# Second norm folded around w_in, w_mod's last columns loaded behind w_in, and wo loaded in plain rows: a cached attention and gMLP decode step

## Chip, cores, metric

One core of a Trainium2 chip runs the whole kernel. The metric is device time in microseconds of one execution; the median over several runs is given, and the profile is of one execution more.

## What is computed

A decode step for four sequences, one token each: an adaptive layer norm, attention over a cache of 4,096 positions in 32 heads, a second adaptive norm and a gated MLP. The shift, scale and gate of each half come from `silu(c) @ w_mod`, six vectors of 512.

```python
def _B_ref(x, w_in, w_sp, b_sp, w_out):
    z = _gelu(jnp.einsum('bsd,df->bsf', x, w_in))
    z1 = z[..., :Fh].copy()
    z2 = _layernorm(z[..., Fh:], axis=-1)
    g = jnp.einsum('ts,bsf->btf', w_sp, z2) + b_sp[None, :, None]
    return jnp.einsum('bsf,fd->bsd', z1 * g, w_out)

x = A_x
mod = (_silu(c) @ w_mod).reshape(c.shape[0], 6, 1, -1)
sa, ca, ga, sb, cb, gb = ...
h = _layernorm(x, axis=-1) * (1 + ca) + sa
x = x + ga * _A_ref(h, A_k_cache, A_v_cache, A_wq, A_wo)
h = _layernorm(x, axis=-1) * (1 + cb) + sb
x = x + gb * _B_ref(h, B_w_in, B_w_sp, B_b_sp, B_w_out)
```

All inputs are bf16. K and V are 4 x 32 x 4,096 x 128 each, 268 MB together; wo is 4,096 x 512, w_in 512 x 1,792, w_out 896 x 512, w_mod 512 x 3,072.

## The kernel before

**Order.** The order of instructions on each engine is that of the code; nothing is rescheduled. Nearly all transfers are issued by SP into one queue, in program order, and a load into a buffer that is still read waits there.

**Quads.** The 32 heads are taken in 8 groups of 4; a group and a sequence make a quad, 32 in all. The K of a quad (4 MB) lies as 128 partitions of 128 positions by 128 elements, and so does its V. Each has two buffers. Loop turn i loads K of quad i+1 and V of quad i, with wo's part for the group (512 KB) between the two at the first sequence of a group (L388). The last quad's K comes in two pieces and its V in four (L96).

**Scores.** DVE multiplies half a K tile by the query in place (L251), PE folds it with 16 matmuls against the identity (L256), DVE reduces and finds the maximum (L265 to L283), ACT takes the exponential (L286).

**Values.** For all quads but the last, PE multiplies V in blocks (L309), ACT copies (L315), PE takes the diagonal (L322). For the last quad, `values_last` has 128 matmuls of a 128x128 V block against four columns (L333) as V's pieces land, with three pairs of filler matmuls between (`keep_busy`, L127). The sum of the weights (`st["z"]`, L295) and the weighted values (`st["o"]`) are two halves of one PSUM tile, `zo`. `project` divides (L344, L345) and writes oT.

**wo.** Seven of the eight loads give each partition four rows in a row (`wo_w`, a run of 4 KB); `apply` then puts oT into that order with 16 small matmuls (L361) and a copy (L367) before it multiplies (L370). The eighth group has one row of 1 KB at a time (`wo_v`) and needs no such step. `apply` stands at the end of the loop turn.

**w_mod.** Vectors 0 and 1 are loaded at the start; 2 to 5 in turn 8 (L402, one load of 2 MB with runs of 4 KB) and multiplied in turn 10 (`mod_part`).

**The tail.** w_in (L431) and w_out (L433) are queued behind the last V. Then: x1 (L436, L437), the sums of x1 and its square by a matmul with a constant matrix (`ln_stats`, L147 to L165: DVE squares, PE sums, DVE takes mean and variance, ACT takes 1/std by Ln and Exp), a table load for GELU (L439), five fillers (L440), the norm in four DVE operations (L442 to L446), 56 matmuls with w_in (L453), one filler, GELU of both halves (L460, L464), a table load, the norm of z2 (`ln_stats` again), 28 matmuls with w_out (L471), the closing arithmetic (L476 to L490), a transposing matmul (L492) and the store (L497).

Of the kernel before, what the change touches and what calls it, by code (L numbers as in the profile page):

```python
# [8 lines left out]
BF16 = mybir.dt.bfloat16  # L9
# [7 lines left out]
def kernel(  # L17
# [75 lines left out]
        return load(A_k_cache, i, "kt", (2, 2) if i == len(quads) - 1 else (1,))  # L93

    def load_v(i):
        return load(A_v_cache, i, "vt", (2, 4, 8, 8) if i == len(quads) - 1 else (1,))  # L96

    NQ = len(quads)

# [22 lines left out]
    def keep_busy(n):  # L122

        if busy_ps[0] is None:
            busy_ps[0] = psum_s.tile([P, 4 * P], F32, name="big", bufs=2)
        for _ in range(n):
            nc.tensor.matmul(busy_ps[0], lhsT=ident, rhs=wide, start=True, stop=True)  # L127
# [40 lines left out]

    modT = persist.tile([P, 6, J, B], F32, name="modT")
    qbc = persist.tile([P, B, G, DH], BF16, name="qbc")  # L170
    x1b = persist.tile([P, 2, J, B], F32, name="x1b")
    wbf = persist.tile([P, 2], F32, name="wbf")
    xcT = persist.tile([P, J, 2 * B], F32, name="xcT")
# [8 lines left out]
        tc.tile_pool(name="psum_s", bufs=1, space=bass.MemoryType.PSUM)  # L182
    )

    def mod_part(wt, w0, oc):
        ps = psum_s.tile([P, J, B], F32, name="small", bufs=1)
        for jo in range(J):
            for j in range(J):
                c0 = (oc - w0) * D + jo * P
                nc.tensor.matmul(  # L190
                    ps[:, jo, :], lhsT=wt[:, j, c0:c0 + P],
                    rhs=sT[:, j, :], start=(j == 0), stop=(j == J - 1),
                )
        if oc in (1, 4):
            nc.vector.tensor_scalar_add(out=modT[:, oc], in0=ps, scalar1=1.0)
        else:
            nc.vector.tensor_copy(out=modT[:, oc], in_=ps)
# [46 lines left out]
    with tc.tile_pool(name="psum_att", bufs=1, space=bass.MemoryType.PSUM) as psum:  # L244
# [47 lines left out]
        def zsum(i):  # L292
            zo = psum.tile([P, 2, NH], F32, name="zo_ps", bufs=2)
            st["z", i], st["o", i] = zo[:, 0], zo[:, 1]
            nc.tensor.matmul(  # L295
                st["z", i], lhsT=ones_f, rhs=rs4s[i % NB], start=True, stop=True,
            )
# [29 lines left out]
        def values_last(i):  # L327
            P4 = P4s[i % NB]
            zsum(i)
            for n in range(NT):  # L330
                if n in (NT // 2, 3 * NT // 4, 7 * NT // 8):
                    keep_busy(2)
                nc.tensor.matmul(  # L333
                    st["o", i], lhsT=st["v", i][:, n, :], rhs=P4[:, n, :],
                    start=(n == 0), stop=(n == NT - 1),
                )

        def project(i):
            g, b = quads[i]
            if b == 0:  # L340
                st["oT", g] = wk.tile([P, NH, B], BF16, name="oT", bufs=2)
            oT = st["oT", g]
            rz = wk.tile([P, NH], F32, name="rz", bufs=2)
            nc.vector.reciprocal(out=rz, in_=st.pop(("z", i)))  # L344
            nc.vector.tensor_tensor(  # L345
                out=oT[:, :, b], in0=st.pop(("o", i)), in1=rz, op=ALU.mult,
            )
            if i == NQ - 1:
                apply(i)

        def apply(i):
            g, b = quads[i]
            if b == B - 1:
                oT = st.pop(("oT", g))
                wo_g = st.pop(("wo", g))
                if g < G - 1:

                    pp = psum_s.tile([P, NH, B], F32, name="small", bufs=1)
                    for r in range(NH):
                        for hl in range(NH):  # L360
                            nc.tensor.matmul(  # L361
                                pp[hl * R:(hl + 1) * R, r, :], lhsT=ident[:, r::NH],
                                rhs=oT[:, hl, :], start=True, stop=True,
                                tile_position=(0, hl * R),
                            )
                    oT = wk.tile([P, NH, B], BF16, name="oP", bufs=2)
                    nc.vector.tensor_copy(out=oT, in_=pp)  # L367
                for hl in range(NH):
                    for jo in range(J):
                        nc.tensor.matmul(  # L370
                            attn_ps[:, jo, :], lhsT=wo_g[:, hl, jo * P:(jo + 1) * P], rhs=oT[:, hl, :],
                            start=(g == 0 and hl == 0 and jo == 0),
                            stop=(g == G - 1 and hl == NH - 1),
                            skip_group_check=True,
                        )


        wo_w = A_wo.rearrange("(g p r) n -> g p r n", p=P, r=NH)
        wo_v = A_wo.rearrange("(g h p) n -> g p h n", h=NH, p=P)
        st["k", 0] = load_k(0)  # L380
        for i in range(NQ + 1):
            if i + 1 < NQ:
                st["k", i + 1] = load_k(i + 1)
            if i < NQ:
                if quads[i][1] == 0:
                    g = quads[i][0]
                    t = wk.tile([P, NH, D], BF16, name="wo_g", bufs=2)
                    nc.sync.dma_start(out=t, in_=(wo_v if g == G - 1 else wo_w)[g])  # L388
                    st["wo", g] = t
                st["v", i] = load_v(i)  # L390
                if i == 0:
                    wq_r = kvp.tile([P, J, (G - 1) * GW], BF16, name="wt", bufs=1)
                    nc.sync.dma_start(out=wq_r, in_=wq_v[:, :, GW:])
                if i in (2, 3):
                    for b in (2 * i - 4, 2 * i - 3):
                        for g0, n in ((1, 3), (4, 4)):
                            qp = psum_s.tile([P, n, DH], F32, name="big", bufs=2)
                            query(wq_r, 1, b, g0, n, qp, 0)
                            nc.scalar.copy(out=qbc[:, b, g0:g0 + n, :], in_=qp)  # L399
                if i == 8:  # L400
                    wm25 = kvp.tile([P, J, 4 * D], BF16, name="wt", bufs=1)
                    nc.sync.dma_start(out=wm25, in_=wmod_v[:, :, 2 * D:])  # L402
                if i == 10:
                    for oc in range(2, 6):
                        mod_part(wm25, 2, oc)
            if i > 1:
                diagonal(i - 2)
            if i < NQ:
# [7 lines left out]
            if i < NQ:  # L416
                fold(i, 0)
                fold(i, 1)
                softmax(i)
            if 1 < i < NQ:  # L420
                apply(i - 2)
        keep_busy(3)
        values_last(NQ - 1)
        project(NQ - 1)
# [1 line left out]

    with tc.tile_pool(name="post", bufs=1) as post, \
            tc.tile_pool(name="psum_post", bufs=1, space=bass.MemoryType.PSUM) as psum:
        wt = kvp.tile([P, J * F + JF * D], BF16, name="wt", bufs=1)
        win = wt[:, 0:J * F].rearrange("p (j n) -> p j n", j=J)  # L430
        nc.sync.dma_start(out=win, in_=B_w_in.rearrange("(j p) n -> p j n", p=P))  # L431
        wout = wt[:, J * F:].rearrange("p (j n) -> p j n", j=JF)
        nc.sync.dma_start(out=wout, in_=B_w_out.rearrange("(p j) n -> p j n", j=JF))  # L433

        x1 = x1b[:, 0]
        nc.vector.tensor_tensor(out=x1, in0=attn_ps, in1=modT[:, 2], op=ALU.mult)  # L436
        nc.vector.tensor_tensor(out=x1, in0=x1, in1=xT, op=ALU.add)  # L437
        mean, rstd = ln_stats(post, psum_s, x1b, mean_d, J, "ln2")
        nc.scalar.preload_act_table_set("gelu_apprx_tanh_and_others")  # L439
        keep_busy(5)  # L440
        h2 = post.tile([P, J, B], F32, name="h2")
        nc.vector.tensor_tensor(out=h2, in0=x1, in1=bc(mean, J), op=ALU.subtract)  # L442
        nc.vector.tensor_tensor(out=h2, in0=h2, in1=bc(rstd, J), op=ALU.mult)
        nc.vector.tensor_tensor(out=h2, in0=h2, in1=modT[:, 4], op=ALU.mult)
        h2T = post.tile([P, J, B], BF16, name="h2T")
        nc.vector.tensor_tensor(out=h2T, in0=h2, in1=modT[:, 3], op=ALU.add)  # L446


        z_ps = psum.tile([P, 2, JF, B], F32, name="zf_ps")
        for s in (1, 0):  # L450
            for jf in range(JF):
                for j in range(J):
                    nc.tensor.matmul(  # L453
                        z_ps[:, s, jf, :], lhsT=win[:, j, s * FH + jf:(s + 1) * FH:JF],
                        rhs=h2T[:, j, :], start=(j == 0), stop=(j == J - 1),
                    )
        keep_busy(1)
        z2b = post.tile([P, 2, JF, B], F32, name="z2b")
        z2 = z2b[:, 0]
        nc.scalar.activation(out=z2, in_=z_ps[:, 1], func=AF.Gelu_apprx_tanh)  # L460


        u = post.tile([P, JF, 2, B], BF16, name="u")
        nc.scalar.activation(out=u[:, :, 1, :], in_=z_ps[:, 0], func=AF.Gelu_apprx_tanh)  # L464
        nc.scalar.preload_act_table_set("natural_log_exp_and_others")
        mean, rstd = ln_stats(post, psum_s, z2b, mean_f, JF, "ln3", lambda:
            nc.vector.tensor_tensor(out=u[:, :, 0, :], in0=u[:, :, 1, :], in1=z2, op=ALU.mult))
# [20 lines left out]
        )  # L488
        yo = post.tile([P, B, J], BF16, name="yo")
        nc.vector.tensor_tensor(out=yo.rearrange("p b j -> p j b"), in0=q, in1=r1, op=ALU.add)  # L490
        t_ps = psum.tile([J * B, P], F32, name="t_ps")
        nc.tensor.matmul(  # L492
            t_ps, lhsT=yo.rearrange("p b j -> p (b j)"), rhs=ident, start=True, stop=True,
        )
# [33 lines left out]
```

## Time and profile before

| | |
|---|---|
| Runs | 675.93, 676.19, 676.55, 676.57; median 676.37 us |
| Profiled execution | 675.76 us, span 674.0 us |
| Instructions | 7,199 |
| Busy: PE / PEld / DVE / ACT | 62% / 31% / 56% / 15% |
| HBM read | 282.73 MB, 419 GB/s over the span |
| Chain that ended last, by engine | DMA 61%, PE 25%, DVE 12% |
| Granted TensorE clock, mean | 0.765 |
| K, V, wo to landing, median | 26.0, 34.3, 25.8 us |

The span is the time from the first instruction to the last of the profiled execution; 1.76 us of its own time lie around it. The median of the runs is 0.61 us above it. PE is TensorE, PEld its weight loads, DVE VectorE, ACT ScalarE, SP the engine that issues transfers; L12 is line 12 of the kernel before.

### The profile page before, as it was taken

The page shows a single profiled execution, that of the slowest core. Times are in us where ns is not written, and L with a number is a line of the kernel's source. Part 1 is how long each engine was busy: PE and PEld are TensorE (multiplying, and loading weights), DVE is VectorE, ACT ScalarE, POOL GpSimd, SP SyncE. Part 2 cuts the span into 40 slices and gives each one's busy share as a digit, 9 for nine tenths or more (in the row PEclk, how much of TensorE's full clock was granted, in tenths as well). Part 3 has the DMA queues.
Part 4 walks back from the last instruction along what each step waited for, and adds up shares of the span by engine and source line. Part 5 has one row for each costly group of instructions (what it writes and reads, how often), then busy time and mean ns, then how long its engine had stood idle before and what let it go on. Part 6 is the DMA issues. An engine that isn't in the chain of part 4 may idle for free.

```text
span 674.0 us, 7199 instructions
## 1 busy us (share of the span) xinstructions
PE 418.7 (62%) x3091; PEld 207.4 (31%) x3095; DVE 376.7 (56%) x408; ACT 102.9 (15%) x311; POOL 4.1 (1%) x18
## 2 busy tenths in 40 slices
PE   2574847765657656567666457765546766555786
PEld 2232423322224222233222223332223322223344
DVE  2665555566653666545656555565645565654732
ACT  1012211101111011111011111101111101111112
POOL 2000000000000000000000000000000000000000
PEclk9976888766778667788767788776678876768885
DMA  9999999999999999999999999999999999999993
GB/s 374 425 418 431 433 435 426 429 432 427 434 431 425 428 429 434 429 433 434 431 424 429 432 433 436 422 434 425 430 433 433 432 431 430 433 422 427 432 409 126
DMA packets 14256, 283.20 MB, mean 420 GB/s; under 512 B 1416, under 2 KB 2448, under 8 KB 5776
## 3 DMA queue, kind: packets, MB, share of 16 engines
q1 hardware_dynamic: 14144, 282.73, 98.2%
q8 instruction: 24, 0.39, 0.2%
q14 instruction: 8, 0.07, 0.0%
q10 hardware_dynamic: 16, 0.01, 0.0%
q0 software_dynamic: 64, 0.00, 0.0%
HBM read 282.73 MB, written 0.00 MB: 419 GB/s over the span
## 4 chain that ended last, share of the span: by engine, by line
DMA 61%; PE 25%; DVE 12%; issue 0%; ACT 0%; SPq 0%; DVEq 0%; ACTq 0%
DMA kt<-in_A_k_cache_dram 61%; PE s_ps L256 23%; DVE kt L251 11%; PE big L127 1%; PE zo_ps L333 0%; PE zf_ps L453 0%; ACT P L286 0%; PE big L309 0%; PE small L149 0%; PE y_ps L471 0%; DVE S L265 0%; ACT osb L315 0%; PE attn_ps L370 0%; PE zo_ps L295 0%; SPq L75 0%
## 5 line engine op out<-in xcount | busy, mean ns | idle before, releaser
L256 PE MATMUL s_ps<-kt,ident 128*128 128x512 bf16 x1024 | 291.9, 455 | 214.1 <-DVE kt L251 214.1
L251 DVE TENSOR_TENSOR kt<-kt,qbc 128x8192 bf16<-128x8192 bf16 x64 | 282.6, 4418 | 127.9 <-DMA kt<-in_A_k_cache_dram 127.9
L256 PEld LDWEIGHTS <-ident 128*128 128x128 bf16 x1024 | 115.7, 113 | 378.0 <-issue 225.0
L265 DVE TENSOR_REDUCE S<-s_ps 128x64 f32<-128x512 f32 x64 | 44.2, 691 | 126.5 <-PE s_ps L256 126.5
L315 ACT COPY osb<-big 128x512 f32<-128x512 f32 x31 | 18.2, 586 | 518.9 <-PE big L309 518.9
L286 ACT ACTIVATE P<-S,nm 32x128 bf16<-32x128 f32 x128 | 73.5, 574 | 20.3 <-DVE nm L283 18.0
L309 PE MATMUL big<-vt,P 128*32 128x512 bf16 x992 | 59.2, 380 | 0.0
L322 PE MATMUL zo_ps<-sel,osb 128*128 128x4 f32 x248 | 33.7, 259 | 16.4 <-ACT osb L315 16.4
L322 PEld LDWEIGHTS zo_ps<-sel,osb 128*128 128x128 f32 x248 | 31.1, 197 | 28.5 <-ACT osb L315 27.3
L286 ACT ACTIVATION_READ_ACCUMULATOR P<-S,nm 32x1 f32 x128 | 31.8, 248 | 0.0
L309 PEld LDWEIGHTS <-P 128*32 128x32 bf16 x992 | 23.7, 96 | 20.8
L295 PEld LDWEIGHTS zo_ps<-rs,ones_f 128*128 128x128 f32 x64 | 12.1, 190 | 5.6 <-ACT P L286 1.2
L204 PE MATMUL big<-wt,hbc 128*32 128x384 bf16 (+1 forms) x128 | 8.5, 404 | 3.8 <-ACT qbc L399 3.7
L344 DVE RECIPROCAL rz<-zo_ps 128x4 f32<-128x4 f32 x32 | 5.6, 176 | 9.1 <-PE zo_ps L333 7.3
L273 DVE TENSOR_REDUCE mx<-S 128x1 f32<-128x128 f32 x32 | 9.2, 286 | 1.3
L295 PE MATMUL zo_ps<-rs,ones_f 128*128 128x4 f32 x64 | 9.1, 212 | 0.7 <-ACT P L286 0.7
L204 PEld LDWEIGHTS <-hbc 128*32 128x32 bf16 x192 | 5.7, 113 | 10.7 <-issue 7.0
L283 DVE STREAM_TRANSPOSE nm<-hb 128x32 f32<-128x32 f32 x32 | 6.8, 212 | 3.2
L275 DVE STREAM_TRANSPOSE mT<-mx 128x32 f32<-128x32 f32 x32 | 6.8, 211 | 1.1
L277 DVE TENSOR_REDUCE hm<-mT 128x1 f32<-128x32 f32 x32 | 6.0, 186 | 1.1
L279 DVE TENSOR_SCALAR hb<-hm 128x32 f32<-128x32 f32 x32 | 5.8, 181 | 1.1
L345 DVE TENSOR_TENSOR oT<-zo_ps,rz 128x4 bf16<-128x4 f32 x32 | 5.4, 168 | 1.1
(92 smaller groups left out, 75.9 us busy)
## 6 DMA issues: line engine op xcount, KB each, us to landing
kt<-in_A_k_cache_dram SPq DMA_DIRECT2D x31, 4096.0 KB, 26.0
vt<-in_A_v_cache_dram SPq DMA_DIRECT2D x31, 4096.0 KB, 34.3
wo_g<-in_A_wo_dram SPq DMA_DIRECT2D x8, 512.0 KB, 25.8
kt<-in_A_k_cache_dram SPq DMA_DIRECT2D x2, 2048.0 KB, 24.2
wt<-in_A_wq_dram SPq DMA_DIRECT2D x1, 3584.0 KB
wt<-in_w_mod_dram SPq DMA_DIRECT2D x1, 2048.0 KB, 38.2
vt<-in_A_v_cache_dram SPq DMA_DIRECT2D x1, 2048.0 KB, 18.9
wt<-in_B_w_in_dram SPq DMA_DIRECT2D x1, 1792.0 KB
```

The source lines that it names most:

```text
L204: nc.tensor.matmul(qp[hl * R:(hl + 1) * R, col:col + n], lhsT=hbc[:, j, b, :], rhs=wv[:, g0 - hl0:g0 - hl0 + n, hl, :], start=(j == 0), st ...
L251: nc.vector.tensor_tensor(out=kt, in0=kt, in1=q[:, None, :].to_broadcast([P, HT, DH]), op=ALU.mult,)
L256: nc.tensor.matmul(ps, lhsT=ident, rhs=kt[:, :, cc * DC:(cc + 1) * DC], start=(cc == 0), stop=(cc == DH // DC - 1),)
L265: nc.vector.tensor_reduce(out=st["S", i][:, half * HT:(half + 1) * HT], in_=st.pop(("s", i, half)), axis=AX.X, op=ALU.add,)
L273: nc.vector.tensor_reduce(out=mx[:, 0:1], in_=S, axis=AX.X, op=ALU.max)
L275: nc.vector.transpose(out=mT, in_=mx)
L283: nc.vector.transpose(out=nm, in_=hb)
L286: nc.scalar.activation(out=P4[rows, 0:NT, hl], in_=S[rows, :], func=AF.Exp, bias=nm[rows, 0:1], scale=att_scale, accum_out=rs4[rows, hl:hl ...
L295: nc.tensor.matmul(st["z", i], lhsT=ones_f, rhs=rs4s[i % NB], start=True, stop=True,)
L309: nc.tensor.matmul(po[32 * t:32 * t + 32], lhsT=P4[:, n0:n0 + 8, :], rhs=st["v", i][:, n0:n0 + 4, :], start=(u == 0), stop=(u == NU - 1), ...
L315: nc.scalar.copy(out=osb, in_=po)
L322: nc.tensor.matmul(st["o", i], lhsT=osb[:, n, :], rhs=sel[:, NH * n:NH * n + NH], start=(n == 0), stop=(n == 3),)
```

## The change

wo is loaded in plain rows for all groups; the permutation goes, and the 16 matmuls with wo move into `project`. The last V comes in five pieces, and its denominator has a PSUM tile of its own. w_mod's vector 5 is no longer loaded in turn 8 but behind w_in, which comes in two halves, the second half of the columns first. The second norm is not applied to h ahead of w_in: w_in is multiplied with three sets of columns, x1(1+scale), 1+scale and shift, and mean and 1/std are applied to the products, `((a - mean*b) * rstd) + c`, for each half. The fillers of the tail go.

```diff
-        return load(A_v_cache, i, "vt", (2, 4, 8, 8) if i == len(quads) - 1 else (1,))
+        return load(A_v_cache, i, "vt", (2, 4, 8, 16, 16) if i == len(quads) - 1 else (1,))
...
+    hx = persist.tile([P, J, 3, B], BF16, name="hx")
...
-    def mod_part(wt, w0, oc):
-        ps = psum_s.tile([P, J, B], F32, name="small", bufs=1)
+    def mod_part(wt, w0, oc, ps=None):
+        if ps is None:
+            ps = psum_s.tile([P, J, B], F32, name="small", bufs=1)
...
             st["z", i], st["o", i] = zo[:, 0], zo[:, 1]
+            if i == NQ - 1:
+                st["z", i] = psum_s.tile([P, NH], F32, name="small", bufs=1)
...
-                if n in (NT // 2, 3 * NT // 4, 7 * NT // 8):
-                    keep_busy(2)
+                if n in (NT // 2, 3 * NT // 4, 7 * NT // 8, 15 * NT // 16):
+                    keep_busy(2 if n < 7 * NT // 8 else 1)
...
-            if i == NQ - 1:
-                apply(i)
-
-        def apply(i):
-            g, b = quads[i]
             if b == B - 1:
-                oT = st.pop(("oT", g))
                 wo_g = st.pop(("wo", g))
-                if g < G - 1:
-
-                    pp = psum_s.tile([P, NH, B], F32, name="small", bufs=1)
-                    for r in range(NH):
-                        for hl in range(NH):
-                            nc.tensor.matmul(
-                                pp[hl * R:(hl + 1) * R, r, :], lhsT=ident[:, r::NH],
-                                rhs=oT[:, hl, :], start=True, stop=True,
-                                tile_position=(0, hl * R),
-                            )
-                    oT = wk.tile([P, NH, B], BF16, name="oP", bufs=2)
-                    nc.vector.tensor_copy(out=oT, in_=pp)
                 for hl in range(NH):
...
-                    nc.sync.dma_start(out=t, in_=(wo_v if g == G - 1 else wo_w)[g])
+                    nc.sync.dma_start(out=t, in_=wo_v[:, g * NH:(g + 1) * NH, :])
...
-                    wm25 = kvp.tile([P, J, 4 * D], BF16, name="wt", bufs=1)
-                    nc.sync.dma_start(out=wm25, in_=wmod_v[:, :, 2 * D:])
+                    wm24 = kvp.tile([P, J, 3 * D], BF16, name="wt", bufs=1)
+                    nc.sync.dma_start(out=wm24, in_=wmod_v[:, :, 2 * D:5 * D])
                 if i == 10:
-                    for oc in range(2, 6):
-                        mod_part(wm25, 2, oc)
+                    for oc in range(2, 5):
+                        mod_part(wm24, 2, oc)
+                    nc.vector.tensor_copy(out=hx[:, :, 1, :], in_=modT[:, 4])
+                    nc.vector.tensor_copy(out=hx[:, :, 2, :], in_=modT[:, 3])
...
-            if 1 < i < NQ:
-                apply(i - 2)
...
-        nc.sync.dma_start(out=win, in_=B_w_in.rearrange("(j p) n -> p j n", p=P))
+        win_v = B_w_in.rearrange("(j p) n -> p j n", p=P)
+        for s in (1, 0):
+            nc.sync.dma_start(
+                out=win[:, :, s * FH:(s + 1) * FH], in_=win_v[:, :, s * FH:(s + 1) * FH],
+            )
+        wm5 = wt[:, J * F + JF * D:].rearrange("p (j n) -> p j n", j=J)
+        nc.sync.dma_start(out=wm5, in_=wmod_v[:, :, 5 * D:])
+        wout = wt[:, J * F:J * F + JF * D].rearrange("p (j n) -> p j n", j=JF)
         nc.sync.dma_start(out=wout, in_=B_w_out.rearrange("(p j) n -> p j n", j=JF))
...
-        mean, rstd = ln_stats(post, psum_s, x1b, mean_d, J, "ln2")
-        nc.scalar.preload_act_table_set("gelu_apprx_tanh_and_others")
-        keep_busy(5)
-        h2 = post.tile([P, J, B], F32, name="h2")
-        nc.vector.tensor_tensor(out=h2, in0=x1, in1=bc(mean, J), op=ALU.subtract)
-        nc.vector.tensor_tensor(out=h2, in0=h2, in1=bc(rstd, J), op=ALU.mult)
-        nc.vector.tensor_tensor(out=h2, in0=h2, in1=modT[:, 4], op=ALU.mult)
-        h2T = post.tile([P, J, B], BF16, name="h2T")
-        nc.vector.tensor_tensor(out=h2T, in0=h2, in1=modT[:, 3], op=ALU.add)
...
+        nc.vector.tensor_tensor(out=hx[:, :, 0, :], in0=x1, in1=hx[:, :, 1, :], op=ALU.mult)
+        zp = {}
+
+        def z_half(s):
+            zp[s] = psum.tile([P, JF, 3, B], F32, name=f"z{s}_ps")
             for jf in range(JF):
                 for j in range(J):
                     nc.tensor.matmul(
-                        z_ps[:, s, jf, :], lhsT=win[:, j, s * FH + jf:(s + 1) * FH:JF],
-                        rhs=h2T[:, j, :], start=(j == 0), stop=(j == J - 1),
+                        zp[s][:, jf], lhsT=win[:, j, s * FH + jf:(s + 1) * FH:JF],
+                        rhs=hx[:, j], start=(j == 0), stop=(j == J - 1),
                     )
-        keep_busy(1)
+
+        def z_norm(s):
+            t = post.tile([P, JF, B], F32, name=f"zn{s}")
+            nc.vector.tensor_tensor(out=t, in0=zp[s][:, :, 1, :], in1=bc(mean, JF), op=ALU.mult)
+            nc.vector.tensor_tensor(out=t, in0=zp[s][:, :, 0, :], in1=t, op=ALU.subtract)
+            nc.vector.tensor_tensor(out=t, in0=t, in1=bc(rstd, JF), op=ALU.mult)
+            nc.vector.tensor_tensor(out=t, in0=t, in1=zp[s][:, :, 2, :], op=ALU.add)
+            return t
+
+
+        z_half(1)
+        mean, rstd = ln_stats(post, psum_s, x1b, mean_d, J, "ln2")
+        nc.scalar.preload_act_table_set("gelu_apprx_tanh_and_others")
+        z_half(0)
+        mod_part(wm5, 5, 5, psum.tile([P, J, B], F32, name="m5_ps"))
...
-        nc.scalar.activation(out=z2, in_=z_ps[:, 1], func=AF.Gelu_apprx_tanh)
+        nc.scalar.activation(out=z2, in_=z_norm(1), func=AF.Gelu_apprx_tanh)
...
-        nc.scalar.activation(out=u[:, :, 1, :], in_=z_ps[:, 0], func=AF.Gelu_apprx_tanh)
+        nc.scalar.activation(out=u[:, :, 1, :], in_=z_norm(0), func=AF.Gelu_apprx_tanh)
...
-        t_ps = psum.tile([J * B, P], F32, name="t_ps")
+        t_ps = psum_s.tile([J * B, P], F32, name="small", bufs=1)
```

More of the change, by code (lines that the diff above doesn't have):

```diff
@@ L375, in apply @@
                         )
-        wo_w = A_wo.rearrange("(g p r) n -> g p r n", p=P, r=NH)
-        wo_v = A_wo.rearrange("(g h p) n -> g p h n", h=NH, p=P)
+        wo_v = A_wo.rearrange("(h p) n -> p h n", p=P)
         st["k", 0] = load_k(0)
@@ L428 @@
             tc.tile_pool(name="psum_post", bufs=1, space=bass.MemoryType.PSUM) as psum:
-        wt = kvp.tile([P, J * F + JF * D], BF16, name="wt", bufs=1)
+        wt = kvp.tile([P, J * F + JF * D + J * D], BF16, name="wt", bufs=1)
         win = wt[:, 0:J * F].rearrange("p (j n) -> p j n", j=J)
-        nc.sync.dma_start(out=win, in_=B_w_in.rearrange("(j p) n -> p j n", p=P))
-        wout = wt[:, J * F:].rearrange("p (j n) -> p j n", j=JF)
+        win_v = B_w_in.rearrange("(j p) n -> p j n", p=P)
[6 more added lines that the diff above has]
+        wout = wt[:, J * F:J * F + JF * D].rearrange("p (j n) -> p j n", j=JF)
         nc.sync.dma_start(out=wout, in_=B_w_out.rearrange("(p j) n -> p j n", j=JF))
@@ L437 @@
         nc.vector.tensor_tensor(out=x1, in0=x1, in1=xT, op=ALU.add)
-        mean, rstd = ln_stats(post, psum_s, x1b, mean_d, J, "ln2")
-        nc.scalar.preload_act_table_set("gelu_apprx_tanh_and_others")
-        keep_busy(5)
-        h2 = post.tile([P, J, B], F32, name="h2")
-        nc.vector.tensor_tensor(out=h2, in0=x1, in1=bc(mean, J), op=ALU.subtract)
-        nc.vector.tensor_tensor(out=h2, in0=h2, in1=bc(rstd, J), op=ALU.mult)
-        nc.vector.tensor_tensor(out=h2, in0=h2, in1=modT[:, 4], op=ALU.mult)
-        h2T = post.tile([P, J, B], BF16, name="h2T")
-        nc.vector.tensor_tensor(out=h2T, in0=h2, in1=modT[:, 3], op=ALU.add)
-        z_ps = psum.tile([P, 2, JF, B], F32, name="zf_ps")
-        for s in (1, 0):
+        nc.vector.tensor_tensor(out=hx[:, :, 0, :], in0=x1, in1=hx[:, :, 1, :], op=ALU.mult)
+        zp = {}
+        def z_half(s):
+            zp[s] = psum.tile([P, JF, 3, B], F32, name=f"z{s}_ps")
             for jf in range(JF):
```

## The prediction

> **What bounds the kernel now.** I read the slices of the page first, then the chain of waits, then the timeline of its last 40 us, then the DMA landings and packets.
>
> ```profile
> DMA  9999999999999999999999999999999999999993
> GB/s 374 425 418 431 433 435 426 429 432 427 434 431 425 428 429 434 429 433 434 431 424 429 432 433 436 422 434 425 430 433 433 432 431 430 433 422 427 432 409 126
> ...
> q1 hardware_dynamic: 14144, 282.73, 98.2%
> ```
>
> The DMA engines are full in 39 of 40 slices at about 430 GB/s, so up to some 655 us time is bytes and packets, and an instruction saved on PE or DVE there is worth nothing. What counts is when the last K and V tiles land and what follows them. The chain, in order of time (start, us, what), shows that:
>
> ```profile
> 591.74 27.34 DMA kt<-in_A_k_cache_dram
> ...
> 653.57 0.39 PE zo_ps L295 x2
> ...
> 659.93 0.20 DVE rz L344
> 660.13 0.02 issue
> 660.15 0.18 DVE oT L345
> ...
> 661.39 0.18 DVE x1b L147
> 661.57 0.04 issue
> 661.62 0.63 PE small L149 x2
> 662.25 2.13 PE big L127 x5
> 664.38 2.96 PE zf_ps L453 x56
> 667.34 0.02 issue
> 667.37 0.20 ACT z2b L460
> 667.57 0.02 issue
> 667.59 0.20 DVE z2b L147
> 667.79 0.04 issue
> 667.84 0.68 PE small L149 x2
> ```
>
> K of the last quad but one lands at 619.08; from there compute runs unbroken to the output. So the sum has two parts: how far the change moves that landing (the whole chain moves with it), and what it does to the tail after 653.57. In the tail the transfers run just ahead of their users: the last V piece lands at 635.7+22.6 = 658.3, w_in at 662.73 (landing event), w_out at 636.64+28.3 = 664.9.
>
> **Rows and packets ahead of the landing.** The packet records give a median of 46 ns for 1,024 B, 84 for 2,048, 142 for 3,584, 160 for 4,096, 1,215 for 32,768; 16 engines work side by side. A load of wo is 512 KB. With 4 KB rows it lands 1.26 to 1.28 us after the K tile ahead of it in the queue (four pairs with nothing between); the eighth load already has 1 KB rows and takes 1.48 (K 598.18, wo 599.66). So each of the seven loads that change costs +0.21, in all +1.47. Packet means (32 x 49.0 against 8 x 161.2 ns per engine) give +0.28 each, +1.96: the upper end; medians give 7 x 0.19 = +1.34, the lower. I take 1.47, the same form measured landing to landing.
>
> w_mod in the middle: 2 MB of 4 KB rows is 32 x 160 ns = 5.1 us per engine; 1.5 MB in 3 KB rows, which no record shows, lies between 84 and 160 ns a packet, on the line between them 122: 32 x 122 = 3.9. That is -1.21 (bounds -2.4 and 0). The landing of K and all behind it moves by +1.47 - 1.21 = **+0.26**. The extra V piece turns 8 packets of 160 into 16 of 84 per engine: +0.06, last V at 658.6.
>
> The Trainium skill, "DMA: Bandwidth & Descriptors", section "Why small descriptors are slow", puts the overhead of a packet at a fixed three or so bus cycles, 32 B a cycle. By that a 1 KB packet loses 3 in 35 and a 4 KB one 3 in 131, and a wo load would grow by only some 0.09 us (an estimate); the sum would be 0.8 us better than mine. The landing at 599.66 says 0.21, and the row decides.
>
> **The permutation that goes.** L361 (112 matmuls) and L367 (7 copies of 0.175) leave PE and DVE; the 16 matmuls of L370 move ahead of the second half's scores. I cost both at nothing: PE is busy 62% under a full queue. They wait on oT (L345), which DVE writes before its second multiplication, while PE still does the first half's matmuls (3.5 us and more). Without that cover it is 16 x 0.026 = 0.4 us in every fourth quad.
>
> **Last V.** Six filler matmuls stay six (2+2+1+1 for 2+2+2), 128 matmuls stay: PE-bound from 653.57 to 659.91, as pieces land before their use (658.3 against 659.3). The denominator in its own bank lets L344 run at 654: the 0.20 of rz with its issue leaves the chain, **-0.22**.
>
> **The tail.** Times in the changed kernel, with +0.26 and -0.22 in. After x1 one more DVE operation, hx, takes the place of L147 in the chain: it starts at 661.43, z_half(1) at 661.66 (0.23 later, as from L147 to L149). Its 28 matmuls go at 53 ns each ((3.12-0.19)/55 from L453): 1.49. Twelve columns for four: L471 with eight goes at 28 ns and L370 with four at 26, so the columns cost little, +0.1 to 0.2 at worst. The sums (L149) stand behind them on PE: 663.15, and z_half(0) starts 0.47 later (as L471 after L149), 663.62, to 665.11. Then mod_part, 16 x 0.026 + 0.16 = 0.58: 665.69. Meanwhile st, msq, var on DVE and two ACT operations end by 665.0. DVE has the copy of modT[5] next in its order, and all of z_norm stands behind it: copy at 665.73, four dependent operations at 0.22 each (L476 to L480) from 665.82, GELU at 666.70, second z_norm from 666.57, GELU at 667.46. DVE squares z2 at 667.32 and PE sums at 667.57. In the profile above PE sums at 667.84: **-0.27** in all, so the tail alone gives -0.31. z2 is earlier by 0.67, u is not: eight DVE operations replaced three and five fillers, and waits for the norm went under matmuls. Behind that nothing changes.
>
> The transfers in it: w_in in two halves of 1,792 B rows, about 75 ns a packet on the line between 46 and 84: 64 x 75 = 4.8 for 32 x 142 = 4.5, so with the 4.44 that w_in took by its landing, 4.66. Halves land at 660.9 and 663.3 (wanted 661.66, 663.62), the last w_mod columns 1.48 later at 664.75 (wanted 665.11), w_out 666.9 (wanted 668.0). All in time, two by 0.35 only.
>
> The fillers at L442's place go too. What covers that: the clock below is at half in the whole stretch although they ran (the columns are busy time and instructions of PE, PEld, DVE, ACT, POOL, then PEclk, DMA share, GB/s).
>
> ```profile
> 654.40:674.00 19.60, 12.97 (x225) 9.78 (x224) 4.22 (x24) 3.85 (x8) 0.00 (x0) 0.50 0.41 164
> ```
>
> GELU now follows its table load more closely. Before, the second load begins at 667.66 and the next ACT operation starts 1.53 later:
>
> ```profile
> 667.66 1.28 ACT L465 ACT_TABLE_LOAD   x1
> ...
> 669.19 0.30 ACT L164 ACTIVATE rstd_ln<-var_ln,eps 128x4 f32<-128x4 f32 x1 [0.24 <-DVE var_ln L162]
> ```
>
> By that row a load begun at 665.0 is over by 666.5, before GELU at 666.70. The Trainium skill, "ScalarE: Activation LUTs", section "What ACT_TABLE_LOAD costs", counts 2.66 us for a switch, a drain included. By it GELU would start at 667.66, and the end would be some 0.4 later than before instead of 0.27 earlier; the row above, where the next operation starts after 1.53, speaks against it.
>
> **Sum.** +0.26 - 0.22 - 0.31 = -0.27: span 674.00 to 673.73, profiled run 675.76 to 675.49. The median shown, 676.37, lies 0.61 over that run, so **676.1**. A measurement of this kernel can't tell less than 0.2%, 1.35 us, from no change: no measurable difference. Its own range is 675.3 to 677.1: wo between 1.34 and 1.96, twelve columns up to +0.2 in each half, the two thin margins of 0.35.
>
> **Rivals.** *B, slower: the last gate's columns come late.* In place: DVE's copy of modT[5] ahead of all of z_norm. It decides once those columns land after 665.1; from there each us of lateness is a us of time. Price with every packet at its worst row: wo +1.96 (landing +0.75), w_in at the 101 ns that 2 KB packets averaged at the kernel's start, 64 x 101 = 6.46, the columns 32 x 56 = 1.79. They land at 658.29+0.81+6.46+1.79 = 667.35, PE is ready at 665.6: 676.37 - 0.53 + 0.75 + 1.75 = **678.3**. For it: three more transfers stand in the queue, and SP sits 10.47 us in one issue there, so the queue takes no more than so much:
>
> ```profile
> 636.64 10.47 SPq L433 DMA_DIRECT2D wt<-in_B_w_out_dram  x1
> ```
>
> If the issue of the late transfers stays behind the drain, they start late too. Against it: a full queue is a busy queue, and that transfer landed in its turn, 2.18 after w_in.
>
> *C, faster: the 1 KB rows cost nothing.* Then only w_mod's -1.21 and the tail count: 676.37 - 1.21 - 0.53 = **674.6**. For it: the whole rate is within 1% in all slices. Against: the 1.48 of the eighth load.
>
> *D, the clock.* PE begins the last K at 638.77 with the clock at half until 644.16. If the changed kernel meets that switch one stretch of 3.4 us earlier or later, it gains or loses half of it: 674.4 or 677.8. Against it: the four runs before lie within 0.64.
>
> **How the numbers follow.** A 0.52, B 0.26, C 0.14, D 0.08 with both signs alike. So faster 0.18, same 0.52, slower 0.30. The time is A's, 676.1. The range 674.7 to 677.9 holds A and D nearly whole and the near parts of B and C, which reach toward A as their conditions hold in part.
>
> **What would show it.** The K landing near 619.3; wo loads at 1.5 us behind K; rz done before L345's wait ends; GELU of z2 near 666.7 and DVE's square near 667.3, with modT[5]'s copy released by PE and PE not by a DMA. It is wrong if mod_part waits for its transfer, if GELU waits for the table, or if K lands outside 618.9 to 619.9.

## The result, and the profile after

The changed kernel takes 676.91 us (median of 39 runs, 676.74 to 677.49) against 675.93 (57 runs, 675.12 to 676.94): a ratio of 1.0015, 95% interval 1.0011 to 1.0020. It is slower by 1.0 us, where 0.3 less was forecast. (The forecast of 676.1 started from a median of four runs, 676.37; from the 675.93 of 57 runs it would read 675.7.) The profiled execution took 676.97, its span 675.1.

The page of the changed kernel, slices, first queue and two of its transfers (KB each, median us from issue to landing):

```profile
DMA  9999999999999999999999999999999999999993
GB/s 373 422 415 434 432 434 418 432 429 430 435 426 418 435 431 430 426 430 430 429 432 427 431 431 424 424 436 433 428 431 420 433 432 433 432 419 426 434 403 138
...
q1 hardware_dynamic: 18032, 282.73, 98.4%
...
wo_g<-in_A_wo_dram SPq DMA_DIRECT2D x8, 512.0 KB, 26.9
...
wt<-in_B_w_in_dram SPq DMA_DIRECT2D x2, 896.0 KB, 24.2
```

The same bytes go in 18,032 packets instead of 14,144, and the engines are as full as before. The chain of waits has changed at its end (start, us, what):

```profile
638.79 24.71 DMA wt<-in_B_w_in_dram
663.50 0.09 issue
663.59 1.63 PE z_ps L439 x28
665.22 0.47 PE small L149 x2
665.69 1.43 PE z_ps L439 x28
667.12 0.43 PE m_ps L193 x16
667.56 0.02 issue
667.58 0.17 DVE modT L200
667.75 0.11 DVE zn L446
...
669.58 0.65 PE small L149 x2
```

Before, the chain ran through compute alone from the landing of the last K but one to the end. Now a transfer, a half of w_in, stands in it just ahead of the first matmuls that use w_in. The timeline of the changed kernel there shows which half:

```profile
662.11 0.17 DVE L432 TENSOR_TENSOR hx<-x1b,hx 128x16 bf16<-128x16 f32 x1
...
663.56 1.57 PEld L439 LDWEIGHTS <-wt 128*128 128x128 bf16 x28 [1.99 <-issue]
663.59 1.63 PE L439 MATMUL z_ps<-hx,wt 128*128 128x12 bf16 x28 [1.93 <-DMA wt<-in_B_w_in_dram]
```

The half that z_half(1) reads was issued at 637.34 and took 23.7 us, so it lay there at 661.07 (landing event). The columns were written at 662.28. PE began at 663.56, and 663.50 = 638.79 + 24.71 is the landing of the other half, of which z_half(1) reads nothing. Between the two, the queue of the weight loads sits in one wait on a semaphore (a counter by which one engine or transfer holds up another), from 662.3 for 1.21 us.

The built program says the same: the first weight load of z_half(1) waits for the semaphores of both loads.

```
SP  82 L418 DMACopy wt_3946<-in_B_w_in_dram 128x4x896 [waits DMAHW3_49]
SP  83 L418 DMACopy wt_3946<-in_B_w_in_dram 128x4x896 [waits DMAHW4_49]
PE  5210 L439 Ldweights wt_3946 [waits DVE_49,DMAHW4_49,DMAHW3_49]
```

(The bracket of a load names its own semaphore's earlier use; the bracket of the weight load names what it waits for.) Each half is four stretches of the tile, one per j, and the other half's stretches lie between them, so from first to last element the two regions overlap. That this is why both loads are waited for is inferred; e1 below tests it.

From PE's sums for z2 to the end the changed profile is 0.6 us shorter than the earlier one (5.6 for 6.1). Some 0.35 of that is a gap ahead of L486 (0.30 us of "issue" at 670.04 in the earlier one). Three of the four profiles with the earlier tail have that gap (before, b_mod, b_nofill; not b_wo), and none of the eight with the changed tail; the rest lies behind the store. No run here shows what makes either.

### The profile page after: what moved, and what is told of

Same layout as the page of the kernel before. It is cut to its first block, busy times and chain, and to the rows that moved or that the text cites. A ratio compares the mean times of both kernels' runs of the same rounds, so it can differ in the third digit from the quotient of the medians.

```text
span 675.1 us, 6969 instructions
## 1 busy us (share of the span) xinstructions
PE 418.1 (62%) x2974; PEld 203.9 (30%) x2977; DVE 376.5 (56%) x408; ACT 103.0 (15%) x311; POOL 4.1 (1%) x18
## 3 DMA queue, kind: packets, MB, share of 16 engines
q1 hardware_dynamic: 18032, 282.73, 98.4%
## 4 chain that ended last, share of the span: by engine, by line
DMA 65%; PE 23%; DVE 11%; issue 0%; SPq 0%; DVEq 0%
DMA kt<-in_A_k_cache_dram 61%; PE s_ps L259 22%; DVE kt L254 11%; DMA wt<-in_B_w_in_dram 4%; PE z_ps L439 0%; PE attn_ps L357 0%; PE small L149 0%; PE y_ps L471 0%; DVE S L268 0%; SPq L75 0%; PE m_ps L193 0%; SPq L71 0%; DVE zn L448 0%; DVE zn L447 0%; DVE zn L449 0%
## 5 line engine op out<-in xcount | busy, mean ns | idle before, releaser
L259 PE MATMUL s_ps<-kt,ident 128*128 128x512 bf16 x1024 | 297.8, 461 | 212.2 <-DVE kt L254 212.2
L300 PEld LDWEIGHTS zo_ps<-rs,ones_f 128*128 128x128 f32 x62 | 11.8, 190 | 4.5
L207 PE MATMUL big<-wt,hbc 128*32 128x384 bf16 (+1 forms) x128 | 7.1, 353 | 3.8 <-ACT qbc L384 3.7
L300 PE MATMUL zo_ps<-rs,ones_f 128*128 128x4 f32 x62 | 8.7, 211 | 0.0
```

The source lines that it names most:

```text
L207: nc.tensor.matmul(qp[hl * R:(hl + 1) * R, col:col + n], lhsT=hbc[:, j, b, :], rhs=wv[:, g0 - hl0:g0 - hl0 + n, hl, :], start=(j == 0), st ...
L259: nc.tensor.matmul(ps, lhsT=ident, rhs=kt[:, :, cc * DC:(cc + 1) * DC], start=(cc == 0), stop=(cc == DH // DC - 1),)
L300: nc.tensor.matmul(st["z", i], lhsT=ones_f, rhs=rs4s[i % NB], start=True, stop=True,)
```

## The experiments

Theory: z_half(1) is held by the second half's landing. Rivals: the late columns and DVE's longer run (rival B of the prediction), the wo rows, the clock. "Spread" is the highest run less the lowest. The kernel before was timed beside each of three groups: 675.80 (e1 to e4), 675.81 (b_wo, b_mod, e6, e7) and 676.01 (e8, b_nofill). No run of the changed kernel is on record in them, so a difference to it, or between groups, can be off by as much as these medians differ, some 0.2 us.

**e1_sep: each half in one stretch.**

```diff
-        win = wt[:, 0:J * F].rearrange("p (j n) -> p j n", j=J)
+        win = {}
         for s in (1, 0):
-            nc.sync.dma_start(
-                out=win[:, :, s * FH:(s + 1) * FH], in_=win_v[:, :, s * FH:(s + 1) * FH],
-            )
+            win[s] = wt[:, s * J * FH:(s + 1) * J * FH].rearrange("p (j n) -> p j n", j=J)
+            nc.sync.dma_start(out=win[s], in_=win_v[:, :, s * FH:(s + 1) * FH])
...
-                        zp[s][:, jf], lhsT=win[:, j, s * FH + jf:(s + 1) * FH:JF],
+                        zp[s][:, jf], lhsT=win[s][:, j, jf::JF],
```

> The changed kernel with the two halves of w_in in two regions of the tile, one behind the other, so that the first matmul needs its own half alone. Theory (the first half's matmuls wait for the landing of both halves, 663.50 in the profile, though their own landed at 661.07 and their columns hx were ready at 662.3): PE starts them when hx is ready, near 662.3, and the time falls by 1.0 to 1.3 us, 676.91 to about 675.7; the spread of the runs grows from 0.75 to about 1.8 us as before the change, because the granted clock ahead of the tail decides again and no transfer. Rival (the last columns of w_mod or the longer run of DVE operations cost the time): nothing moves, 676.9.

Measured: 675.46 (11 runs, spread 1.07), ratio to before 0.9993 (0.9984 to 1.0002). The loss is gone: 1.45 us below the changed kernel, or 1.32 with each against the kernel before of its own group. The spread grew less than expected, to 1.07 instead of 1.8. The order of its program: weight load 5210 waits for DMAHW3 alone, DMAHW4 has moved to 5267, the first of z_half(0). The timeline of this kernel:

```profile
661.64 0.17 DVE L431 TENSOR_TENSOR hx<-x1b,hx 128x16 bf16<-128x16 f32 x1
661.73 0.17 DVE L147 TENSOR_TENSOR x1b<-x1b 128x16 f32<-128x16 f32 x1
661.93 1.57 PEld L438 LDWEIGHTS <-wt 128*128 128x128 bf16 x28 [0.83 <-DMA wt<-in_B_w_in_dram]
661.96 1.63 PE L438 MATMUL z_ps<-hx,wt 128*128 128x12 bf16 x28 [0.78 <-DVE x1b L147]
663.39 0.53 PEld L149 LDWEIGHTS small<-x1b,mean_d 128*128 128x128 f32 x2
```

The wait on a semaphore ahead of the weight loads takes 0.05 us instead of 1.21. PE starts 0.32 after hx begins (1.48 in the changed kernel), at 661.96, while the second half still lands at 663.50, the same moment as before this edit. That shows the cause: same transfers at the same times, another wait.

**e2_one: w_in in one load.**

```diff
-        for s in (1, 0):
-            nc.sync.dma_start(
-                out=win[:, :, s * FH:(s + 1) * FH], in_=win_v[:, :, s * FH:(s + 1) * FH],
-            )
+        nc.sync.dma_start(out=win, in_=win_v)
```

> The changed kernel with w_in in one load, rows of 3,584 B. Theory (both halves are waited for anyway): the one load lands some 0.2 us earlier than the second half did, 676.7, spread still under 1 us. Rival (the early half does let PE start ahead): PE then starts later than with halves, 677.5 or more.

Measured: 676.68 (spread 0.34), as the theory has it: splitting the load as the change does buys nothing. It costs 0.2 by the medians (0.1 with each against its group's kernel before); w_in in one load lands at 663.11 instead of 663.50.

**e3_wo4 and e4_sep_wo4: wo in four rows again.** e3 puts `apply`, `wo_w` and the permutation back into the changed kernel, as in the code before; e4 does that on top of e1.

> The changed kernel with wo in runs of four rows again, with the permutation, for seven groups. Theory (each 1 KB load costs 0.2 us of the queue, and the end hangs on a landing): the landing of w_in comes 1.3 to 1.5 us earlier and the time falls as much, to 675.5. Rival (the rows cost nothing, the transfers have slack): 676.9.

> Both edits: halves in two regions and wo in runs of four rows. Theory: the two gains add, since compute and transfers both move with the K landing: 676.91 - 1.2 - 1.4 = 674.3. Rival: no more than the better of the two alone, 675.5.

Measured: e3 675.27 (spread 0.33; 1.64 below the changed kernel, 1.5 by each group's kernel before), e4 673.94 (9 runs, spread 1.77; 1.52 below e1), ratio to before 0.9972 (0.9963 to 0.9982). The rows cost 1.5 to 1.6 us in both; the two gains add. In e3 the half of w_in lands at 661.88 and PE starts at 661.97: still held, only earlier.

**b_wo and b_mod: the two DMA terms on the kernel before.** b_wo loads wo in plain rows and drops the permutation. b_mod moves vector 5 to between the last V and w_in (the change has it behind w_in), and its matmuls replace the five fillers:

```diff
-                    nc.sync.dma_start(out=wm25, in_=wmod_v[:, :, 2 * D:])
+                    nc.sync.dma_start(out=wm24, in_=wmod_v[:, :, 2 * D:5 * D])
...
+        wm5 = wt[:, J * F + JF * D:].rearrange("p (j n) -> p j n", j=J)
+        nc.sync.dma_start(out=wm5, in_=wmod_v[:, :, 5 * D:])
         nc.sync.dma_start(out=win, in_=B_w_in.rearrange("(j p) n -> p j n", p=P))
...
-        keep_busy(5)
+        mod_part(wm5, 5, 5, psum.tile([P, J, B], F32, name="m5_ps"))
```

> The kernel before with wo in plain rows for all groups and without the permutation, nothing else changed. Theory: seven loads cost 0.21 us of the queue each, K and all behind it move, +1.47 us: 675.8 to 677.3. Rival (the queue has slack, or the saved permutation pays): no change.

> The kernel before with w_mod's vector 5 loaded between the last V and w_in, and its 16 matmuls in place of the five fillers behind the second norm's sums. Theory: 0.5 MB less ahead of K, -1.2 us, w_in lands when it did (662.7) and is still early enough: 674.6. It also tells whether the five fillers did anything: if they held up the clock, the w_in matmuls take longer than 2.96 us and the gain is smaller. Rival (the late transfer eats what it saves): no change, 675.8.

Measured: b_wo 677.10, +1.29, ratio 1.0019 (1.0010 to 1.0028). Its profile is of its slowest run, 677.88, and there K lands at 621.48, 2.4 later than before, so the median is the better measure. b_mod 675.00, -0.81, ratio 0.9987 (0.9978 to 0.9996): a third less than expected. In its profile K lands at 617.88, 1.20 earlier than before, as worked out; but w_in stays at 663.04 and PE's loads wait for it until 663.08, 0.14 before the norm is ready:

```profile
663.08 3.15 PEld L456 LDWEIGHTS <-wt 128*128 128x128 bf16 x56 [1.41 <-DMA wt<-in_B_w_in_dram]
663.22 3.10 PE L456 MATMUL zf_ps<-h2T,wt 128*128 128x4 bf16 x56 [1.46 <-DVE h2T L449]
```

An execution whose compute comes out earlier than in this profile would meet the transfer, which would cut off part of the gain; that this makes the missing third is argued, not shown. The 56 matmuls take 3.10 here and 3.12 with the five fillers: those fillers did nothing for the clock.

**e6_copy: DVE's copy of modT[5] behind z_norm.** e4, with the `mod_part` call moved behind the second GELU.

> Halves in two regions, wo in four rows, and DVE's copy of modT[5] behind both z_norm instead of ahead of them. In the profile of the kernel without this edit the copy begins at 665.32 and the first z_norm follows at once, though its products were there at 663.0 and 1/std at 664.6. Theory (the copy holds up z_norm): GELU moves up until the table load (664.64 + 1.28) ends, the square and PE's sums by 0.7 to 0.9 us: 673.94 to about 673.1. Rival (z_norm is held by its own products): no change.

Measured: 673.45 (5 runs, spread 1.67), 0.49 below e4 by medians that both scatter; from hx to PE's sums the profiles have 6.32 (661.00 to 667.32) and 5.52 (660.59 to 666.11), 0.80 less. The timeline of e6 shows the first z_norm ending at 664.64 and GELU held by the table load instead:

```profile
664.22 1.28 ACT L475 ACT_TABLE_LOAD   x1
...
664.46 0.18 DVE L469 TENSOR_TENSOR zn<-zn,z_ps 128x28 f32<-128x28 f32 x1
...
665.32 0.17 DVE L200 COPY modT<-m_ps 128x16 f32<-128x16 f32 x1
665.52 0.23 ACT L479 ACTIVATE z2b<-zn 128x28 f32<-128x28 f32 x1
```

GELU begins 1.30 after its load does. The 2.66 us that the Trainium skill ("ScalarE: Activation LUTs", "What ACT_TABLE_LOAD costs") counts for a switch would have held it until 666.88; here the load's own 1.28 is all that shows.

**e7_copy_nofill, e8_nofill, b_nofill: no fillers among the last products.**

```diff
-                if n in (NT // 2, 3 * NT // 4, 7 * NT // 8, 15 * NT // 16):
-                    keep_busy(2 if n < 7 * NT // 8 else 1)
```

> Halves in two regions and wo in four rows, with the copy where the change has it, and without the six fillers among the last quad's matmuls. Theory (the clock is at half there with the fillers, so they only take 0.43 us each): the last products end when the last V piece lands, 657.7 plus 0.4, 1.6 us earlier, and the second half of w_in, 662.28, then holds PE: the time falls by 0.9 us to 673.0 and the spread by more than half. Rival (the fillers hold the clock up later in the tail): no gain or slower.

> Halves in two regions, wo in four rows, the copy of modT[5] where the change has it, and no fillers among the last quad's matmuls (e7_copy_nofill, by a slip, had the copy behind z_norm as well). Theory: the products end with the last V piece, the second half of w_in (lands near 662.1) holds PE, and 673.94 falls by 0.9 us to 673.0 with a spread under 1 us. Rival (the fillers hold the clock up): no gain.

> The kernel before without the six fillers among the last quad's matmuls. Theory: the products end 1.4 to 1.6 us earlier, the norm too, and then w_in (lands at 662.7) holds the 56 matmuls that began at 664.2: 675.8 to about 674.5, spread from 1.8 us to under 1, as a transfer and no longer the clock decides. Rival: no gain or slower, the fillers keep the clock up.

The kernel of e7 has the copy behind z_norm, other than its expectation says; it is read against e8. Measured: e8 673.44 (5 runs, spread 0.41), 0.50 below e4 where 0.9 was expected. e7 672.44 (5 runs, spread 0.78), 0.9950 (0.9937 to 0.9962) of before and 1.00 below e8, or 0.80 by each group's kernel before. With PE's start fixed by a transfer in both, that is the price of the copy in front of z_norm with the 16 matmuls that it waits for; from that transfer's landing to the end the profiles have 9.73 (e8) and 8.69 (e7). b_nofill 674.89 (spread 0.65), -1.12, ratio 0.9986 (0.9977 to 0.9995). The timeline of e7 has the queue holding PE at each piece:

```profile
657.47 0.29 PEld L336 LDWEIGHTS <-vt 128*128 128x128 bf16 x8 [0.39 <-DMA vt<-in_A_v_cache_dram]
...
659.86 1.57 PEld L457 LDWEIGHTS <-wt 128*128 128x128 bf16 x28 [1.27 <-DMA wt<-in_B_w_in_dram]
...
662.13 1.57 PEld L457 LDWEIGHTS <-wt 128*128 128x128 bf16 x28 [0.27 <-DMA wt<-in_B_w_in_dram]
```

In b_nofill it is not w_in that decides, as I had expected: it landed at 662.91, and the norm's last operation began at 663.11. The last piece of V does, with the norm and its fillers after it (chain of waits of b_nofill):

```profile
636.05 22.42 DMA vt<-in_A_v_cache_dram
658.47 0.05 issue
658.51 0.60 PE zo_ps L331 x16
...
661.68 1.91 PE big L127 x4
663.60 2.96 PE zf_ps L451 x56
```

e7 beats both kernels: 4.5 us below the change, 3.4 below the kernel before.

## Why the prediction was wrong

The step that failed is one sentence on the transfers in the tail: "Halves land at 660.9 and 663.3 (wanted 661.66, 663.62)". The landings were right, 661.07 and 663.50. "Wanted" was not: z_half(1) wants both. I took it that a matmul waits for the data it reads, and did not ask which loads the program would make it wait for. With both halves needed at 661.66 and the second expected at 663.3, the same numbers give 1.6 more in the tail, and a sum of +1.4 instead of -0.27; measured, PE started 1.16 later after hx than in e1, and the change cost 1.0. The signs that the prediction listed could not show this: K landed in its range, PE released the copy and no table load held GELU, but none of them asked when z_half(1) starts.

Undoing that wait alone (e1) gives 675.46, 0.34 below before; forecast without it, 0.27 below. That near agreement is partly luck. From the denominator's matmuls (L295, in the change L300) to PE's sums for z2 the tail became shorter by 0.11 (e1) and 0.35 (e4), where 0.53 was forecast, and the stretch behind, where nothing was to change, became shorter by 0.6. The interval of e1 against before reaches from 1.1 below to 0.1 above.

The other steps, by their own terms:

| Term | Forecast | Measured |
|---|---|---|
| wo in 1 KB rows | +1.47 | +1.29 on the kernel before, 1.5 to 1.6 taken back from the change; landing behind K 1.37 to 1.44 in its profile, for 1.26 to 1.28 |
| w_mod's vector 5 out of the middle, K landing | -1.21 | -1.20 (b_mod) |
| K landing of the change | +0.26 | +0.18 (619.08 to 619.26); but b_nofill, with the loads of before up to there, has 619.26 too |
| Last V; columns; w_out land | 658.6; 664.75; 666.9 | 658.74; 664.88; 667.05 |
| rz out of the chain | -0.22 | from L295 (L300) to L147, or to hx, 7.82 before, 7.59 in the change, 7.60 in e4; 7.85 in e1, whose L300 took 0.20 longer |
| hx to z_half(1) | 0.23 | 0.32 (e1) |
| z_half(1) | 1.49 | 1.49 (e1), twelve columns for four |
| hx to the copy | 4.30 | 4.31 (e1) |
| Copy to PE's sums | 1.84 | 2.00 (e1) |
| Behind PE's sums | 0 | -0.6 (5.6 for 6.1) |

- *Rival B* named the copy ahead of z_norm as the place. The columns landed at 664.88, two us before PE came to them, so lateness was not the price. But the place was a price all the same: the copy and its matmuls ahead of z_norm cost 0.8 to 1.0 us (e7 against e8) even with their data there. I had that inside the sum without seeing it as a choice of order.
- *Rival C* falls: the 1 KB rows cost 1.3 to 1.6, about what the eighth load said.
- *Rival D*, the clock: in the changed profile it came back at 645.37 instead of 644.16, and PE's 32 products of the last K ended 0.95 later. The wait for w_in hid it.
- *Table load and fillers*: the row was right in both (e6; b_mod, b_nofill).
- *The bound for no change*: 0.2% was too coarse. With 39 and 57 runs the interval is 0.05% to either side, and it tells a loss of 1.0 us from none.

## What to carry to other kernels

A load that is split so that work can start on its first part may not help if the parts interleave in the buffer, as here: read the waits of the built program, not the data that an instruction needs. In a kernel whose queue is full to the end, list for every late transfer when it lands and when it is wanted, and count each 512 KB load by its packets. And an operation that waits for something late must not stand ahead of others in its engine's order: the copy of a gate that is needed at the very end held up a whole norm for 0.8 to 1.0 us.

## What the runs showed beside that

The spread of the runs goes with what holds the end, over sets of 5 to 57 runs. Where a transfer does, it is 0.33 to 0.78 (e2, e3, e7, e8, b_nofill; the change 0.75 in 39 runs); where compute does, 1.07 to 1.82 (before 1.82 in 57 runs; e1, e4, b_wo, e6). b_mod, where w_in comes 0.14 ahead of the norm, has 0.89. Profiles suggest why: the 32 products of the last K took 8.59 us with the clock back 3.1 us after they began (e1), 9.71 with 5.4 (before), 9.97 with 5.9 (the change). That the clock makes the whole spread is argued, not shown.

The six fillers among the last products cost 1.1 us in the kernel before and bought no clock: it was at half behind them with and without (0.50 over 660 to 670 in the kernel before and in e7).

SP's issue of the second half of w_in took 12.25 us, as w_out's had taken 10.47, and that of the columns 4.19. The transfers landed in their turn all the same: the second half of w_in 2.43 us behind the first, the columns 1.38 behind that, w_out 2.17 behind them.
